# A spectral filter and a gated MLP on one core: loads on one queue, a gated spin, two-step roots, an inverse ordered by pairs

## The chip, the core and the metric

The kernel runs on one core of a Trainium2 chip. The metric is the device time of one execution in microseconds (us), as the median of several runs. TensorE (PE, with its weight loads PEld), VectorE (DVE), ScalarE (ACT), GpSimd (POOL) and SyncE (SP) each run their own instructions in a fixed order and wait for each other through semaphores. Loads and stores are DMAs; here SP, ACT and POOL issue them.

## The reference

```python
def reference(A_x, A_w_r, A_w_i, B_x, B_w_gate, B_w_up, B_w_down):
    x = A_x                                    # (1, 2048, 512), bf16
    xn = _layernorm(x, axis=-1)                # (x - mean) / sqrt(var + 1e-5)
    # A: irfft2(rfft2(xn) * (w_r + 1j * w_i)) over the two last axes
    # B: (gelu_tanh(xn @ w_gate) * (xn @ w_up)) @ w_down, inner width 1792
    return x + A + B
```

The comments stand for the bodies of two inner functions. All tensors are bf16.

## The kernel before, in words

The 2,048 tokens lie on 128 partitions with 16 tokens each; token `16 p + c` is partition p, column c. A "column" below is one c, that is 128 tokens of 512 values. Columns 0 to 3 form block 0, and so on to block 3.

**Layernorm.** Each column needs `bn_stats` and `bn_aggr` on DVE (L325, L328), a reciprocal root, and the normalised column `xn`. Columns 0 and 1 (`first_two`, L371) use ACT's square root and DVE's reciprocal, and are normalised in halves of 256 on DVE (L331). Columns 2 and 3 (`second_two`) run a root of Newton steps on DVE (`rsqrt_steps`, L342): two operations for a start value from the bits of the number, then three steps of three dependent operations. The later columns come four at a time (`later_four`): the same steps with four operations each on POOL, then ACT normalises (L449).

**Transposes.** Columns 0 to 3 are transposed on PE against the identity (L337) into PSUM and copied to `xnT` by DVE (L340). Columns 4 to 15 are transposed by DMAs on SP (L452).

**The MLP.** `unit` (L464) makes a gate product `g_ps` and an up product `u_ps` of four accumulating matmuls each (L483) for one 128-wide slice fc of the inner width and 1, 2 or 4 columns; ACT applies gelu (L488), DVE multiplies (L493, into `hT`). Columns 0 and 1 are done one at a time for fc 0 to 3, columns 0-1 and 2-3 in pairs after that, everything else in fours. `g_ps` and `u_ps` have two PSUM buffers each.

**The spectral part.** Four folds per block on DVE (L534, L540) feed 16 small matmuls against `RF_t` (`bp`, L552). Eight groups follow (`group`): matmuls `dp` and `ep`, a chain of DVE products with the filter (`TW`), an exchange of halves by four DMAs per group on SP (L702), and matmuls `gp` (L711). `inverse` (L736) takes pairs of columns: `yp` on PE (L742), a copy on ACT (L748), two sums `lv` and two `yt` on DVE (L754, L759).

**The end.** `down` (L776) accumulates 14 matmuls against `Wd_sb` (L787) and one of `yt` against `RI_t` (L791) into `y_ps` for each column; DVE adds x (L794), SP stores.

**What sets the order.** Loads are issued first, as written in L274 to L302: SP takes most of them, ACT takes the first three parts of the up weights and columns 2-3. Each load has one of eight semaphores in turn, so a load waits until the one eight places before it has landed. Then 37 spin matmuls on zeros are pinned at PE's head (L309). All later work goes through a planner (`Plan`, L124): each operation has an engine, an occupancy, a latency, dependencies, a key and buffers taken and given back; it is placed at the earliest modelled time. `LAND`, `W_LAND` and `RF_LAND` are the planner's assumed landing times. Only the order of each engine's instructions comes from it; the waits are those of the data and buffers.

Of the kernel before, what the change touches and what calls it, by code (L numbers as in the profile page):

```python
# [10 lines left out]
P = 128  # L11
# [10 lines left out]
NE = 4  # L22
# [3 lines left out]
EPS = 1e-5  # L26
N_SPIN = 37

# [93 lines left out]


class Op:  # L124
    __slots__ = ("eng", "occ", "lat", "fn", "deps", "key", "slack", "t_min", "acq", "rel", "start", "done", "n",
# [8 lines left out]
class Plan:  # L134
# [13 lines left out]
    def order(self):  # L148
        left = {}
        for op in self.ops:  # L150
            left.setdefault(op.eng, []).append(op)
        for ops in left.values():
            ops.sort(key=lambda o: (o.key, o.n))
        free = dict.fromkeys(left, 0.0)
        taken = dict.fromkeys(self.room, 0)
        back = {r: [] for r in self.room}
        out = []

        def start_of(op):
            if op.after is not None and op.after.start is None:  # L160
                return None
            t = max(free[op.eng], op.t_min)
            for d in op.deps:
                if d.done is None:
                    return None
                t = max(t, d.done + op.slack)
            for r in op.acq:
                over = taken[r] + 1 - self.room[r]
                if over > len(back[r]):
                    return None  # L170
                if over > 0:
                    t = max(t, sorted(back[r])[over - 1])
            return t

        while any(left.values()):
            best = None
            for eng, ops in left.items():
                pick = None
                for op in ops:
                    t = start_of(op)  # L180
                    if t is not None and (pick is None or t < pick[0] - 1e-6):
                        pick = (t, op)
                        if t <= free[eng] + 1e-6:
                            break
                if pick and (best is None or pick[0] < best[0]):
                    best = pick
            assert best, [(o.eng, o.key) for ops in left.values() for o in ops[:2]]
            t, op = best
            op.start, op.done = t, t + op.lat
            free[op.eng] = t + op.occ  # L190
            for r in op.acq:
                taken[r] += 1
            for r in op.rel:
                back[r].append(op.done)
            left[op.eng].remove(op)
            out.append(op)
        return out
# [3 lines left out]
def kernel(  # L201
# [74 lines left out]
    load_consts("ident", "ident")  # L276
    load_w(Wg_sb, 0, 256)
    load_w(Wg_sb, 256, 512)
    load_w(Wg_sb, 512, 1024)
    pin(load_w(Wu_sb, 0, 256, nc.scalar))  # L280
    pin(load_w(Wu_sb, 256, 512, nc.scalar))
    pin(load_x(2, 2, nc.scalar))
    pin(load_w(Wu_sb, 512, 1024, nc.scalar))
    load_x(4, 4)
    nc.sync.dma_start(out=RF_t[:], in_=rf_d.rearrange("p (c k) -> p c k", c=NC))
    load_w(Wg_sb, 1024, DF)
    load_w(Wu_sb, 1024, DF)
    load_x(8, 4)
    load_x(12, 4)
    load_consts("F0", "M0")  # L290
    LAND = {0: 3.0, 1: 3.4, 2: 7.4, 3: 7.4}
    LAND.update({c: 14.0 if c < 8 else 22.0 if c < 12 else 23.5 for c in range(4, NC)})
    W_LAND = [5.2] * 2 + [6.6] * 2 + [9.6] * 4 + [20.5] * 6
    RF_LAND, CT_LAND, TW_LAND = 15.5, 25.5, 29.0

# [11 lines left out]

    sp_ps = ps.tile([P, P], F32, name="sp_ps", tag="S", bufs=4)
    for _ in range(N_SPIN):  # L309
        pin(nc.tensor.matmul(sp_ps[:], lhsT=spin[:], rhs=spin[:], start=True, stop=True))  # L310

# [11 lines left out]
    def f_stats(c):  # L323
        tiles["st", c] = st = pw.tile([P, V.BN_STATS_DIM], F32, name="stats", bufs=3)
        V.bn_stats(out=st[:], in_=x_t[:, c, :])  # L325
# [12 lines left out]

    def f_Tc(c, e0, n):
        V.tensor_copy(out=xnT[0][:, e0:e0 + n, c, :], in_=tiles["T", c, e0][:])  # L340

    def rsqrt_steps(U, c0, n):  # L342
# [4 lines left out]
        def first():  # L347
            U.tensor_scalar(out=v[:], in0=mv[:, c0:c0 + n, 1], scalar1=EPS, scalar2=None, op0=ALU.add)
            U.tensor_scalar(out=y.bitcast(I32), in0=v[:].bitcast(I32), scalar1=-0.5, scalar2=float(0x5F3759DF),
                            op0=ALU.mult, op1=ALU.add)  # L350

        def newton():
            U.tensor_tensor(out=t[:], in0=y, in1=y, op=ALU.mult)
            if U is V:
                U.scalar_tensor_tensor(out=t[:], in0=v[:], scalar=-0.5, in1=t[:], op0=ALU.mult, op1=ALU.mult)
                U.scalar_tensor_tensor(out=y, in0=t[:], scalar=1.5, in1=y, op0=ALU.add, op1=ALU.mult)
                return
            U.tensor_tensor(out=t[:], in0=v[:], in1=t[:], op=ALU.mult)
            U.tensor_scalar(out=t[:], in0=t[:], scalar1=-0.5, scalar2=1.5, op0=ALU.mult, op1=ALU.add)
            U.tensor_tensor(out=y, in0=t[:], in1=y, op=ALU.mult)  # L360
# [5 lines left out]

        return [first, newton, newton, newton] + ([] if U is V else [bias])

    xn_op, xT_op = {}, {}

    def first_two():  # L371
        o = {}

        def v(k, fn, occ, deps=(), lat=None, t_min=0.0):
            o[k] = add("DVE", occ, fn, [o[d] for d in deps], key=-2000 + len(o), lat=lat, t_min=t_min)

# [5 lines left out]
        def T(c, h):  # L382
            o["T", c, h] = add("PE", 0.12, lambda: f_T(c, 2 * h, 2), [o["xn", c, h]], key=-2000 + 2 * c + h,
                               lat=0.4, acq=("S",))

# [18 lines left out]
        mean(0)  # L404
        stats(1)
        recip(0)
        xn_(0, 0)
        xn_(0, 1)
        mean(1)
        T(0, 0)  # L410
        T(0, 1)
        copy(0, 0)
        copy(0, 1)
        recip(1)
        xn_(1, 0)
# [12 lines left out]
    def moments(c, key):  # L428
        s = add("DVE", 0.7, lambda: f_stats(c), key=key, t_min=LAND[c], lat=0.7)
        return add("DVE", 0.1, lambda: f_mean(c), [s], key=key - 0.5)  # L430

    def second_two():
        m = [moments(c, -900 + c) for c in (2, 3)]
        for k, f in enumerate(rsqrt_steps(V, 2, 2)):
            m = [add("DVE", 0.4, f, m, key=-890 + k, lat=0.4)]
        for c in (2, 3):
            xn_op[c] = add("DVE", 0.33, lambda c=c: f_norm_v(c, 0, D), m, key=-880 + c)
            t = add("PE", 0.23, lambda c=c: f_T(c, 0, NE), [xn_op[c]], key=-880 + c, lat=0.5, acq=("S",))
            xT_op[c] = add("DVE", 0.34, lambda c=c: f_Tc(c, 0, NE), [t], key=-880 + c, rel=("S",))

    second_two()

    def later_four(c0, km, kx):
        m = [moments(c, km + 0.1 * c) for c in range(c0, c0 + 4)]
        for k, f in enumerate(rsqrt_steps(nc.gpsimd, c0, 4)):
            m = [add("POOL", (0.8, 1.15, 1.15, 1.15, 0.7)[k], f, m, key=c0 + k,
                     lat=(0.8, 1.15, 1.15, 1.15, 0.9)[k])]
        for c in range(c0, c0 + 4):
# [15 lines left out]
    def unit(k, c0, n, fc):  # L464
# [25 lines left out]
        def f_h():  # L490
            if alloc:
# [5 lines left out]
        g = add("PE", occ, lambda: mm("g_ps", "G", Wg_sb), src, key=1000 + k, lat=occ + 0.3, acq=("G",),  # L497
                t_min=W_LAND[fc])
        u = add("PE", occ, lambda: mm("u_ps", "U", Wu_sb), src, key=1000.5 + k, lat=occ + 0.3, acq=("U",),
                t_min=W_LAND[fc])  # L500
        ge = add("ACT", {1: 0.28, 2: 0.36, 4: 0.5}[n], f_ge, [g, table], key=-1000 + k,
# [98 lines left out]
    def group(i, g):  # L600
# [24 lines left out]
        for h in range(2):  # L625
            m = pe(0.224, lambda h=h: dp(h), bs_ops, kk + h, acq=("S",))
            m.t_min = 55.0 + 5.6 * i
            d = add("ACT", 0.5, lambda h=h: ds(h), [m], key=ka + 0.1 * h, acq=("ds",), rel=("S",))
# [98 lines left out]
    def load_ri():  # L727
        late["yt"] = pc.tile([P, NC, D], BF16, name="yt", tag="Bs")
        late["RI"] = pc.tile([P, NC, P], BF16, name="RI_t", tag="RF")
        nc.sync.dma_start(out=late["RI"][:], in_=ri_d.rearrange("p (c k) -> p c k", c=NC))  # L730

    ri = add("SP", 0.4, load_ri, gs_ops[-1:], key=300, lat=6.0)
    wd = add("SP", 0.4, lambda: nc.sync.dma_start(out=Wd_sb[:], in_=wd_v), key=50, lat=12.0, t_min=70.0)
    yt_op = {}

    def inverse(c0):  # L736
# [19 lines left out]

        def y(s):
            o = slice(511, 255, -1) if s else slice(0, 256)
            V.tensor_tensor(out=late["yt"][:, c0:c0 + 2, o], in0=b["lv"][:, :, 0], in1=b["lv"][:, :, 1],  # L759
                            op=ALU.subtract if s else ALU.add)  # L760

        d = []
        for j in range(2):
            m = pe(0.224, lambda j=j: yp(j), gs_ops, 1965 + 10 * (c0 + j), acq=("S",))
            d.append(add("ACT", 0.5, lambda j=j: yf(j), [m], key=60 + c0 + j, acq=() if j else ("E",), rel=("S",),
                         after=d[0] if d else None))
        d = [add("DVE", 0.35, lambda: lv(0), d + [ri], key=60 + c0, lat=0.35, acq=("X",))]
        d = [add("DVE", 0.42, lambda: lv(1), d, key=60 + c0 + 0.1, lat=0.42, rel=("E",))]
# [79 lines left out]
```

## Time and profile before

| what | us |
|---|---|
| median of three runs | 184.84 |
| lowest and highest of them | 184.56, 185.5 |
| the profiled execution's own time | 184.4 |
| its span, first to last instruction | 182.5 |
| PE busy | 174.2 (95%) |
| DVE busy | 119.0 (65%) |
| ACT busy | 96.5 (53%) |
| mean granted PE clock | 0.988 |

"Busy" is the union of an engine's instructions. Ends of matmuls are modelled and reach into the next ones, so a gap in PE's busy time is a little shorter than the time lost; starts of successive matmuls give the true rate. A wait is an idle stretch of an engine with what ended it. A line of a timeline gives start, length, engine, line of the kernel, operation, what it writes and reads, shapes, how many instructions are merged, and in brackets the idle time before it and who ended it. The granted clock is the share of PE's full clock. SPq and ACTq are the issuing of DMAs; their last number is the time from issue to landing. For this kernel the 40 slices of the page are 4.56 us each.

### The profile page before, as it was taken

How to read it: one execution, taken by the hardware profiler on the slowest of the kernel's cores; microseconds unless marked ns; L12 is line 12 of the kernel's file. 1: busy time of each engine (PE TensorE's matmuls, PEld its weight loads, DVE VectorE, ACT ScalarE, POOL GpSimd, SP SyncE). 2: the span in 40 equal slices, each digit the busy share in tenths (PEclk: the TensorE clock that was granted, in tenths of full speed). 3: DMA queues.
4: the chain of work that ended last, by engine and by line, in shares of the span. 5: the costliest groups of instructions: out<-in, count | busy, mean ns of one | idle time of the engine just before them, and what ended most of it. 6: DMA issues, size and time to landing. Idle time of an engine off the chain costs nothing.

```text
span 182.5 us, 3172 instructions
## 1 busy us (share of the span) xinstructions
PE 174.2 (95%) x1124; PEld 96.9 (53%) x1124; DVE 119.0 (65%) x279; ACT 96.5 (53%) x181; POOL 22.8 (12%) x68
## 2 busy tenths in 40 slices
PE   7497999999999999989999999999999999999993
PEld 7396774555455455545555545455544544544462
DVE  1687999895483499798999979637354254254221
ACT  3442437988947889988999965355211211121000
POOL 0000075588760000000000000000000000000000
PEclk9889999999999999999999999999999999999998
DMA  5999931442970002952211520230042222222221
GB/s 146 311 394 382 354 97 33 84 86 48 201 189 0 0 4 59 304 155 58 51 37 41 135 59 4 60 114 4 0 134 67 83 67 83 73 71 86 66 70 40
DMA packets 22208, 19.39 MB, mean 106 GB/s; under 512 B 8304, under 2 KB 20720, under 8 KB 22192
## 3 DMA queue, kind: packets, MB, share of 16 engines
q1 hardware_dynamic: 20048, 16.56, 30.3%
q0 software_dynamic: 416, 1.32, 3.1%
q10 hardware_dynamic: 1728, 1.31, 2.3%
q8 instruction: 9, 0.15, 0.3%
q14 instruction: 7, 0.06, 0.1%
HBM read 13.41 MB, written 2.10 MB: 85 GB/s over the span
## 4 chain that ended last, share of the span: by engine, by line
PE 82%; DMA 11%; DVE 4%; issue 1%; SPq 0%; DVEq 0%
PE y_ps L787 27%; PE u_ps L483 23%; PE g_ps L483 22%; DMA Wu_sb<-in_B_w_up_dram 6%; DMA F<-F 3%; DMA x_t<-in_A_x_dram 2%; PE yp L742 2%; PE bp L552 2%; PE gp L711 2%; PE y_ps L791 2%; DVE hT L493 2%; PE dp L608 1%; PE ep L617 1%; DVE xnT L340 0%; DVE m L658 0%
## 5 line engine op out<-in xcount | busy, mean ns | idle before, releaser
L483 PE MATMUL u_ps<-xnT,Wu_sb 128*128 128x512 bf16 (+2 forms) x272 | 59.2, 345 | 1.0 <-DMA Wu_sb<-in_B_w_up_dram 1.0
L483 PE MATMUL g_ps<-xnT,Wg_sb 128*128 128x512 bf16 (+2 forms) x272 | 59.5, 347 | 0.3 <-DVE xnT L340 0.3
L493 DVE TENSOR_TENSOR hT<-u_ps,ge 128x512 bf16<-128x512 f32 (+2 forms) x68 | 39.9, 592 | 20.1 <-PE u_ps L483 12.4
L787 PE MATMUL y_ps<-Wd_sb,hT 128*128 128x512 bf16 (+1 forms) x238 | 51.1, 366 | 0.0
L488 ACT ACTIVATE ge<-g_ps 128x512 bf16<-128x512 f32 (+2 forms) x68 | 35.6, 525 | 26.9 <-PE g_ps L483 22.8
L483 PEld LDWEIGHTS <-Wg_sb 128*128 128x128 bf16 x272 | 25.8, 101 | 21.2 <-DVE xnT L340 0.6
L483 PEld LDWEIGHTS <-Wu_sb 128*128 128x128 bf16 x272 | 25.5, 100 | 21.6 <-DMA Wu_sb<-in_B_w_up_dram 1.3
L787 PEld LDWEIGHTS <-hT 128*128 128x128 bf16 x238 | 22.8, 98 | 22.4
L794 DVE TENSOR_TENSOR y_sb<-y_ps,y_sb 128x512 bf16<-128x512 f32 (+1 forms) x17 | 11.1, 660 | 30.5 <-PE y_ps L791 30.5
L748 ACT CAST yf<-yp 128x512 bf16<-128x512 f32 x16 | 9.1, 589 | 34.4 <-PE yp L742 32.3
L622 ACT CAST E<-ep 64x512 bf16<-64x512 f32 x32 | 18.5, 579 | 1.5 <-PE ep L617 1.1
L325 DVE BATCH_NORM_STATS2 stats<-x_t 128x6 f32<-128x512 bf16 x16 | 10.7, 672 | 4.7 <-DMA x_t<-in_A_x_dram 4.7
L449 ACT ACTIVATE xn<-x_t,nb,rstd 128x512 bf16<-128x512 bf16 x12 | 9.4, 819 | 2.2 <-POOL nb L365 2.2
L522 ACT CAST Gs<-gp 128x512 bf16<-128x512 f32 x16 | 9.0, 594 | 1.0 <-PE gp L711 0.9
L522 ACT CAST ds<-dp 128x512 bf16<-128x512 f32 x16 | 9.0, 597 | 0.0
L522 ACT CAST Bs<-bp 128x512 bf16<-128x512 f32 x16 | 8.2, 604 | 0.0
L754 DVE TENSOR_TENSOR lv<-yf 128x512 bf16<-128x512 bf16 x16 | 6.1, 421 | 1.3 <-ACT yf L748 0.6
L742 PEld LDWEIGHTS <-Gs 128*128 128x128 bf16 x64 | 4.7, 98 | 3.1
L711 PEld LDWEIGHTS <-F 128*128 128x128 bf16 x64 | 4.4, 98 | 3.5 <-DMA F<-F 1.0
L759 DVE TENSOR_TENSOR yt<-lv 128x512 bf16<-128x512 bf16 x16 | 6.1, 421 | 0.3
L791 PE MATMUL y_ps<-yt,RI_t 128*128 128x512 bf16 (+1 forms) x17 | 6.1, 366 | 0.0
L711 PE MATMUL gp<-CT,F 128*128 128x128 bf16 x64 | 5.5, 219 | 0.5 <-DMA F<-F 0.5
(64 smaller groups left out, 124.9 us busy)
## 6 DMA issues: line engine op xcount, KB each, us to landing
F<-F SPq DMA_DIRECT2D x32, 64.0 KB, 2.0
y_sb<-in_A_x_dram SPq DMA_DIRECT2D x16, 128.0 KB, 2.1
out_dram<-y_sb SPq DMA_DIRECT2D x15, 128.0 KB, 1.7
Wd_sb<-in_B_w_down_dram SPq DMA_DIRECT2D x1, 1792.0 KB, 8.4
x_t<-in_A_x_dram SPq DMA_DIRECT2D x3, 512.0 KB, 11.0
Wg_sb<-in_B_w_gate_dram SPq DMA_DIRECT2D x1, 768.0 KB, 10.3
Wu_sb<-in_B_w_up_dram SPq DMA_DIRECT2D x1, 768.0 KB, 10.1
Wu_sb<-in_B_w_up_dram ACTq DMA_DIRECT2D x2, 256.0 KB, 4.7
```

The source lines that it names most:

```text
L325: V.bn_stats(out=st[:], in_=x_t[:, c, :])
L449: xn_op[c] = add("ACT", 0.72, lambda c=c: A.activation(out=xn[:, c, :], in_=x_t[:, c, :], func=AF.Identity, bias=nb[:, c:c + 1], scale=rst ...
L483: T_.matmul(b[name][:], lhsT=W_[:, e, fc * P:(fc + 1) * P], rhs=rhs[:, e, :], start=(e == 0), stop=(e == NE - 1))
L488: A.activation(out=b["ge"][:], in_=b["g_ps"][:], func=AF.Gelu_apprx_tanh)
L493: V.tensor_tensor(out=hT[sb, fc][:, o:o + w], in0=b["u_ps"][:], in1=b["ge"][:], op=ALU.mult)
L522: A.copy(out=o, in_=i)
L622: A.copy(out=b["E"][64 * h:64 * h + 64, r], in_=b["ep", h][64 * r:64 * r + 64])
L711: T_.matmul(t[:, q], lhsT=b["F2"][:, h, q % 2, q // 2::2], rhs=cc("M" if 2 * g + h else "M0"), start=(q == 0), stop=(q == 3), skip_group_c ...
L748: A.copy(out=b["yf"][:, j], in_=b[j][:])
L787: T_.matmul(b[o][:], lhsT=hT[sb, f][:, cl * P:(cl + 1) * P], rhs=Wd_sb[:, f, o:o + w], start=(f == 0), stop=False)
L791: T_.matmul(b[o][:], lhsT=late["RI"][:, c, :], rhs=late["yt"][:, c, o:o + w], start=False, stop=True)
L794: V.tensor_tensor(out=b["y"][:, o:o + w], in0=b[o][:], in1=b["y"][:, o:o + w], op=ALU.add)
```

## The change

1. All opening loads are issued by SP: columns 0, 1, the identity, columns 2-3, then gate and up weights in alternating parts, then columns 4-7, the rest of the weights, columns 8-11, `RF_t`, columns 12-15 and the constants. ACT issues none. `RF_t` moves behind columns 8-11. The planner's assumed landing times change with it.
2. The 37 spin matmuls of 128 columns become 20 of them and 5 of 512 columns that read column 0 of x.
3. The reciprocal root has two steps (other constants) in place of three, on DVE and on POOL.
4. In `first_two`, DVE's order is fixed: statistics and mean of column 0, the same of column 1, then the reciprocals and normalisations. Copies of transposed columns 2 and 3 go to ACT. `bn_stats` results have four buffers, not three.
5. The planner counts a dependency on the same engine by the engine's occupancy (PE, DVE) and not by latency.
6. `RI_t` is loaded after the last `bp` has been copied, not after the last `gp`; the buffer of `yt` is taken when `yt` is first written.
7. `yp` of both columns of the first pair have one key; those of later pairs have keys 20 higher, so each later `yp` stands two columns later on PE than before. In the resulting order the second `yp` of a pair stands just ahead of the 14 matmuls of the pair's first column.

Without the spin both programs have the same 1,087 matmuls.

```diff
-N_SPIN = 37
+SAME = {"PE": 0.0, "DVE": 0.09}
...
-                t = max(t, d.done + op.slack)
+                t = max(t, d.start + d.occ + SAME[op.eng] if d.eng == op.eng and d.eng in SAME else d.done + op.slack)
...
     load_consts("ident", "ident")
-    load_w(Wg_sb, 0, 256)
-    load_w(Wg_sb, 256, 512)
-    load_w(Wg_sb, 512, 1024)
-    pin(load_w(Wu_sb, 0, 256, nc.scalar))
-    pin(load_w(Wu_sb, 256, 512, nc.scalar))
-    pin(load_x(2, 2, nc.scalar))
-    pin(load_w(Wu_sb, 512, 1024, nc.scalar))
+    load_x(2, 2)
+    for f0, f1 in ((0, 256), (256, 512), (512, 1024)):
+        load_w(Wg_sb, f0, f1)
+        load_w(Wu_sb, f0, f1)
     load_x(4, 4)
-    nc.sync.dma_start(out=RF_t[:], in_=rf_d.rearrange("p (c k) -> p c k", c=NC))
     load_w(Wg_sb, 1024, DF)
     load_w(Wu_sb, 1024, DF)
     load_x(8, 4)
+    nc.sync.dma_start(out=RF_t[:], in_=rf_d.rearrange("p (c k) -> p c k", c=NC))
     load_x(12, 4)
...
-    sp_ps = ps.tile([P, P], F32, name="sp_ps", tag="S", bufs=4)
-    for _ in range(N_SPIN):
-        pin(nc.tensor.matmul(sp_ps[:], lhsT=spin[:], rhs=spin[:], start=True, stop=True))
+    sp_ps = ps.tile([P, D], F32, name="sp_ps", tag="S", bufs=4)
+    for k in range(25):
+        pin(nc.tensor.matmul(sp_ps[:, :P if k < 20 else D], lhsT=spin[:], rhs=spin[:] if k < 20 else x_t[:, 0, :],
+                             start=True, stop=True))
...
-        return [first, newton, newton, newton] + ([] if U is V else [bias])
+        steps = [first, lambda: newton(0.703952253, 0.703952253 * 2.38924456), lambda: newton(0.5, 1.5)]
+        return steps + ([] if U is V else [bias])
...
         stats(0)
         mean(0)
         stats(1)
+        mean(1)
         recip(0)
         xn_(0, 0)
         xn_(0, 1)
-        mean(1)
+        recip(1)
         T(0, 0)
         T(0, 1)
         copy(0, 0)
         copy(0, 1)
-        recip(1)
...
-            xT_op[c] = add("DVE", 0.34, lambda c=c: f_Tc(c, 0, NE), [t], key=-880 + c, rel=("S",))
+            xT_op[c] = add("ACT", 0.5, lambda c=c: f_Tc(c, 0, NE, A.copy), [t], key=-1100 + c, rel=("S",))
...
-    ri = add("SP", 0.4, load_ri, gs_ops[-1:], key=300, lat=6.0)
+    ri = add("SP", 0.4, load_ri, bs_ops[-1:], key=300, lat=6.0, t_min=60.0)
...
-            m = pe(0.224, lambda j=j: yp(j), gs_ops, 1965 + 10 * (c0 + j), acq=("S",))
+            m = pe(0.224, lambda j=j: yp(j), gs_ops, 1985 + 10 * (c0 + j) if c0 else 1990, acq=("S",))
...
-        d = [add("DVE", 0.35, lambda: lv(0), d + [ri], key=60 + c0, lat=0.35, acq=("X",))]
+        d = [add("DVE", 0.35, lambda: lv(0), d, key=60 + c0, lat=0.35, acq=("X",))]
```

More of the change, by code (lines that the diff above doesn't have):

```diff
@@ L288 @@
     load_x(8, 4)
+    nc.sync.dma_start(out=RF_t[:], in_=rf_d.rearrange("p (c k) -> p c k", c=NC))
     load_x(12, 4)
     load_consts("F0", "M0")
[L291 to L294, printed above, removed]
+    LAND = {0: 3.0, 1: 3.4, 2: 4.3, 3: 4.3}
+    LAND.update({c: 12.6 if c < 8 else 18.5 if c < 12 else 21.5 for c in range(4, NC)})
+    WG_LAND = [5.2] * 2 + [7.0] * 2 + [9.5] * 4 + [15.0] * 6
+    WU_LAND = [6.1] * 2 + [7.9] * 2 + [11.0] * 4 + [17.0] * 6
+    RF_LAND = 20.0
     idx_t = pc.tile([P, 3], I32, name="idx_t")
@@ L323, in f_stats @@
     def f_stats(c):
-        tiles["st", c] = st = pw.tile([P, V.BN_STATS_DIM], F32, name="stats", bufs=3)
+        tiles["st", c] = st = pw.tile([P, V.BN_STATS_DIM], F32, name="stats", bufs=4)
         V.bn_stats(out=st[:], in_=x_t[:, c, :])
@@ L337, in f_T, with f_Tc @@
             T_.transpose(tp[:, e], xn[:, c, (e0 + e) * P:(e0 + e + 1) * P], ident)
-    def f_Tc(c, e0, n):
-        V.tensor_copy(out=xnT[0][:, e0:e0 + n, c, :], in_=tiles["T", c, e0][:])
+    def f_Tc(c, e0, n, copy=V.tensor_copy):
+        copy(out=xnT[0][:, e0:e0 + n, c, :], in_=tiles["T", c, e0][:])
     def rsqrt_steps(U, c0, n):
@@ L348, in first, with newton @@
             U.tensor_scalar(out=v[:], in0=mv[:, c0:c0 + n, 1], scalar1=EPS, scalar2=None, op0=ALU.add)
-            U.tensor_scalar(out=y.bitcast(I32), in0=v[:].bitcast(I32), scalar1=-0.5, scalar2=float(0x5F3759DF),
+            U.tensor_scalar(out=y.bitcast(I32), in0=v[:].bitcast(I32), scalar1=-0.5, scalar2=float(0x5F1FFFF9),
                             op0=ALU.mult, op1=ALU.add)
-        def newton():
+        def newton(a, k):
             U.tensor_tensor(out=t[:], in0=y, in1=y, op=ALU.mult)
             if U is V:
-                U.scalar_tensor_tensor(out=t[:], in0=v[:], scalar=-0.5, in1=t[:], op0=ALU.mult, op1=ALU.mult)
-                U.scalar_tensor_tensor(out=y, in0=t[:], scalar=1.5, in1=y, op0=ALU.add, op1=ALU.mult)
+                U.scalar_tensor_tensor(out=t[:], in0=v[:], scalar=-a, in1=t[:], op0=ALU.mult, op1=ALU.mult)
+                U.scalar_tensor_tensor(out=y, in0=t[:], scalar=k, in1=y, op0=ALU.add, op1=ALU.mult)
                 return
             U.tensor_tensor(out=t[:], in0=v[:], in1=t[:], op=ALU.mult)
-            U.tensor_scalar(out=t[:], in0=t[:], scalar1=-0.5, scalar2=1.5, op0=ALU.mult, op1=ALU.add)
+            U.tensor_scalar(out=t[:], in0=t[:], scalar1=-a, scalar2=k, op0=ALU.mult, op1=ALU.add)
             U.tensor_tensor(out=y, in0=t[:], in1=y, op=ALU.mult)
@@ L374, in v @@
         def v(k, fn, occ, deps=(), lat=None, t_min=0.0):
-            o[k] = add("DVE", occ, fn, [o[d] for d in deps], key=-2000 + len(o), lat=lat, t_min=t_min)
+            o[k] = add("DVE", occ, fn, [o[d] for d in deps], key=-2000 + len(o), lat=lat, t_min=t_min,
+                       after=o.get("last"))
+            o["last"] = o[k]
         def root_of(c):
@@ L383, in T @@
             o["T", c, h] = add("PE", 0.12, lambda: f_T(c, 2 * h, 2), [o["xn", c, h]], key=-2000 + 2 * c + h,
-                               lat=0.4, acq=("S",))
+                               lat=0.36, acq=("S",))
         def recip(c):
@@ L428, in moments @@
     def moments(c, key):
-        s = add("DVE", 0.7, lambda: f_stats(c), key=key, t_min=LAND[c], lat=0.7)
+        s = add("DVE", 0.6, lambda: f_stats(c), key=key, t_min=max(LAND[c], 6.4))
         return add("DVE", 0.1, lambda: f_mean(c), [s], key=key - 0.5)
@@ L434, in second_two @@
         for k, f in enumerate(rsqrt_steps(V, 2, 2)):
-            m = [add("DVE", 0.4, f, m, key=-890 + k, lat=0.4)]
+            m = [add("DVE", 0.4, f, m, key=-890 + k, lat=0.42)]
         for c in (2, 3):
@@ L445, in later_four @@
         for k, f in enumerate(rsqrt_steps(nc.gpsimd, c0, 4)):
-            m = [add("POOL", (0.8, 1.15, 1.15, 1.15, 0.7)[k], f, m, key=c0 + k,
-                     lat=(0.8, 1.15, 1.15, 1.15, 0.9)[k])]
+            m = [add("POOL", (0.8, 1.15, 1.15, 0.7)[k], f, m, key=c0 + k,
+                     lat=(0.8, 1.15, 1.15, 0.9)[k])]
         for c in range(c0, c0 + 4):
@@ L497, in unit @@
         g = add("PE", occ, lambda: mm("g_ps", "G", Wg_sb), src, key=1000 + k, lat=occ + 0.3, acq=("G",),
-                t_min=W_LAND[fc])
+                t_min=WG_LAND[fc])
         u = add("PE", occ, lambda: mm("u_ps", "U", Wu_sb), src, key=1000.5 + k, lat=occ + 0.3, acq=("U",),
-                t_min=W_LAND[fc])
+                t_min=WU_LAND[fc])
         ge = add("ACT", {1: 0.28, 2: 0.36, 4: 0.5}[n], f_ge, [g, table], key=-1000 + k,
@@ L626, in group @@
             m = pe(0.224, lambda h=h: dp(h), bs_ops, kk + h, acq=("S",))
-            m.t_min = 55.0 + 5.6 * i
+            m.t_min = 54.0 + 5.5 * i
             d = add("ACT", 0.5, lambda h=h: ds(h), [m], key=ka + 0.1 * h, acq=("ds",), rel=("S",))
@@ L727, in load_ri @@
     def load_ri():
-        late["yt"] = pc.tile([P, NC, D], BF16, name="yt", tag="Bs")
         late["RI"] = pc.tile([P, NC, P], BF16, name="RI_t", tag="RF")
         nc.sync.dma_start(out=late["RI"][:], in_=ri_d.rearrange("p (c k) -> p c k", c=NC))
-    ri = add("SP", 0.4, load_ri, gs_ops[-1:], key=300, lat=6.0)
+    ri = add("SP", 0.4, load_ri, bs_ops[-1:], key=300, lat=6.0, t_min=60.0)
     wd = add("SP", 0.4, lambda: nc.sync.dma_start(out=Wd_sb[:], in_=wd_v), key=50, lat=12.0, t_min=70.0)
@@ L757, in y @@
         def y(s):
+            if s + c0 == 0:
+                late["yt"] = pc.tile([P, NC, D], BF16, name="yt", tag="Bs")
             o = slice(511, 255, -1) if s else slice(0, 256)
```

## The prediction

> **What bounds the kernel now.** I read the page's engine rows first, then who waited for whom, then TensorE's and VectorE's timelines of the first 19 us, the stretches, and the DMA issues.
>
> ```profile
> PE 174.2 (95%) x1124; PEld 96.9 (53%) x1124; DVE 119.0 (65%) x279; ACT 96.5 (53%) x181; POOL 22.8 (12%) x68
> PE   7497999999999999989999999999999999999993
> DVE  1687999895483499798999979637354254254221
> ```
>
> TensorE (PE) is the bound, with holes only in the first four slices, one in slice 18 and the store at the end.
>
> ```profile
> PE tp L337 <- DVE xn L331: 2.4, 1, 2.4
> PE u_ps L483 <- DMA Wu_sb<-in_B_w_up_dram: 1.0, 1, 1.0
> PE gp L711 <- DMA F<-F: 0.5, 1, 0.5
> PE g_ps L483 <- DVE xnT L340: 0.3, 1, 0.3
> ```
>
> These are all of PE's waits after the spin; the stretches show where the clock is lost as well (columns: length, PE busy, granted clock, DMA):
>
> ```profile
> 7.03:10.86 3.83, 3.77 (x34) 0.56 1.04 359
> 10.86:18.77 7.91, 6.59 (x82) 1.00 1.05 389
> 18.77:80.00 61.23, 61.23 (x392) 1.00 0.45 117
> 80.00:81.50 1.50, 1.00 (x14) 1.00 0.01 3
> 81.50:179.30 97.80, 97.80 (x573) 1.00 0.22 65
> ```
>
> So outside the opening only 80 to 81.5 us has room. The opening in order:
>
> ```profile
> 0.98 3.68 PE L310 MATMUL sp_ps<-spin 128*128 128x128 bf16 x37 [0.98 <-DVE eps_t L263]
> 3.10 0.69 DVE L325 BATCH_NORM_STATS2 stats<-x_t 128x6 f32<-128x512 bf16 x1 [2.17 <-DMA x_t<-in_A_x_dram]
> 5.24 0.69 DVE L325 BATCH_NORM_STATS2 stats<-x_t 128x6 f32<-128x512 bf16 x1 [1.45 <-DMA x_t<-in_A_x_dram]
> 5.85 0.30 DVE L328 BATCH_NORM_AGGREGATE mv<-stats 128x2 f32<-128x6 f32 x2
> 6.64 0.84 DVE L331 TENSOR_SCALAR xn<-x_t,mv,rstd 128x256 bf16<-128x256 bf16 x3
> 7.03 1.36 PE L337 MATMUL tp<-CT,xn 128*128 128x128 bf16 x8 [2.37 <-DVE xn L331]
> 8.18 0.63 PE L483 MATMUL g_ps<-xnT,Wg_sb 128*128 128x128 bf16 x4
> 15.64 1.05 PE L483 MATMUL u_ps<-xnT,Wu_sb 128*128 128x256 bf16 x8 [1.00 <-DMA Wu_sb<-in_B_w_up_dram]
> ```
>
> Column 0's mean is queued behind column 1's statistics, and these wait for a load that lands at 5.24; so PE has nothing from 4.66 to 7.03. The clock then drops and the first matmuls take 107 ns per 128 columns.
>
> **PE's account.** The order of instructions of both kernels holds the same 1,087 matmuls besides the spin: 336 of 128 columns, 126 of 256, 625 of 512. At full clock, start to start, they take 55.5 ns (16 in 0.89), 109 ns and 215.8 ns (14 in 3.02): 18.6 + 13.7 + 134.9 = 167.3 us. From 7.03 that would end at 174.3; the last one ends its issue at 179.2. Lost after the first transpose: 4.9 us. It splits so: first transpose to first g, 1.15 less 0.44 of work = 0.7; half clock from 8.18 to 10.86, 25 matmuls too long by 51 ns = 1.3; the wait for the up weights 1.2 (the view's 1.0 counts from a modelled end); the wait for xnT 0.5 and small ones 0.1; the exchange at 80.6 in two steps 0.9; evacuation before y_ps at 124.7, 0.2.
>
> **First columns.** x0, x1, ident, x2-3 and the weights now go out in this order on SP alone. With SP's issue spacing of 0.43 us, x1 should land half a microsecond after x0, not 2.1. Bounds for x0: no later than 3.08 as now; no earlier than about 2.5, by when 128 KB would have moved at the present total rate (26 KB to 2.0, then 193 KB in one us). Statistics, mean, root now run per column: statistics of column 1 from about 3.5 to 3.9, +0.6 statistics, +0.15 mean, +0.25 reciprocal to xn, +0.39 to the first transpose (6.64 to 7.03): 4.9 to 5.35, I take 5.1. The gated spin costs nothing before that: 20 cold matmuls fill 0.98 to 3.1, five of 512 columns at 0.43 end at 5.25 if all are cold and near 4.7 if the clock rises at 4.0. Bounds 0 to 0.2. Gain 7.03 - 5.1 = 1.9.
>
> **Clock.** The row first: PE stood idle 2.37 us and the clock was 0.50 from about 7.45 to 10.86. The Trainium skill, "TensorE: Matmul & The Clock Gate", Part 1, says throttling takes an idle window of about 3.4 us. By that rule the present gap shouldn't have cooled the array, the longer spin would be worth nothing, and my sum would lose 1.2 us. The trace shows cooling after a window that was about 30% busy (0.6 of spin, 0.4 of transposes), while the one holding the stall at 14.7 to 15.6, about 70% busy, kept the clock. In the changed kernel the gap shrinks to under 1.5 us with transposes inside, so any 3.4 us is some 60 to 70% busy: I side with the row and take 0.1 of cold loss (bounds 0 and 1.3). Gain 1.2.
>
> **Weights.**
>
> ```profile
> Wg_sb<-in_B_w_gate_dram SPq DMA_DIRECT2D x1, 512.0 KB, 8.0
> Wu_sb<-in_B_w_up_dram ACTq DMA_DIRECT2D x1, 512.0 KB, 10.4
> ```
>
> Issued at 5.24, the up half landed at 15.6. The skill's "DMA: Bandwidth & Descriptors", Queues, rings and completion order, says each DMA engine takes turns between queues by packet; that fits an ACT queue of 1 KB rows trickling beside SP's 4 KB rows[...]. By the rates of each us in the trace (cumulative 0.48 MB at 4, 1.07 at 6, 1.67 at 8, 2.39 at 10, 2.80 at 11, 3.98 at 14, 4.73 at 16) the new order lands x2-3 near 4.3, up columns 0-255 at 6.0, to 511 at 7.7, to 1023 at 10.6, the rest at 16. PE asks for them at about 6.2, 7.7, 11.4 and 22. If 512-byte rows alone in one queue run at 250 GB/s instead of 300, the first two slip by up to 1 us. I take 0.15 of the 1.2 as left: gain 1.05.
>
> **VectorE (DVE) in the opening.** This is what is late next. From the first g at 5.8 until columns 2-3 are normalised it must do, start to start: 2 statistics 1.2, 4 copies 0.8, 2 xn halves 0.4, 8 hT of 128 columns 1.7, 2 means 0.2, 8 dependent root steps 1.6 (0.2 each as at 12.15 to 14.19; the third Newton step's 0.6 is gone), 2 xn 0.6: 6.5, to 12.2. PE's own work up to the transposes of 2-3 (16 + 4 groups, 8 transposes) is 5.7, to 11.5. In the order, statistics stand ahead of two hT products three times, and u matmuls wait for a PSUM buffer behind them: walking both queues I get waits of 0.1 to 0.3, in all 0.9, and PE's first 512-column group at 21.6 with 14.9 of work behind it. Bounds: 0.5 (the present 0.5 + 0.1, DVE being equally loaded then) to 2.0. Against the present 0.6 this is 0.3 worse. The two copies moved to ACT (0.41 each there on DVE) and the lost Newton step are in this sum. After that DVE, 97 to 99% busy from 18.8 to 32 us now, gets earlier by its idle pieces now filled (1.45, 1.09, 0.96) and 1.3 of work taken off: 4.8, enough for PE's lead of about 4.1, with margins of 0.5 to 1 us. I add 0.1.
>
> **Things at no cost.** POOL's shorter roots (1.1 us less per group of four) bring ACT's xn and the DMA transposes forward; PE reaches xnT1 at about 33.8, transposes issued from about 23, 6.4 us in all, are done before; without that cover they'd cost their lag. ACT gets two 0.5 us copies and loses four issues; it has 3 us idle there. RF and constants land by 19 and 21, used at 25. RI now waits on SP for the last bp matmul (near 48), ahead of the first exchange (near 65): 3.7 us of loading, hidden. The fourth stats buffer removes waits only.
>
> **Exchange at 80.6.**
>
> ```profile
> 69.28 2.44 SPq L702 DMA_DIRECT2D F<-F  x4
> 71.77 0.59 SPq L733 DMA_DIRECT2D Wd_sb<-in_B_w_down_dram  x1
> 75.15 2.40 SPq L702 DMA_DIRECT2D F<-F  x4
> ```
>
> The second exchange waits behind Wd (8.4 us). SP's order is unchanged there, so all of it comes 4 us earlier, but its gp now stands at 70.3 us of PE work instead of 69.0: 1.3 us of cover for a loss of 0.9. Left 0.2 (bounds 0 and 0.9): gain 0.7.
>
> **Inverse by pairs.** Each second yp comes just before a block of 14 y_ps. From yp's end (131.7) to the pair's last yt (134.14) it now takes 2.5 us; the matmul that needs it comes after 3.02 + 0.22 = 3.24. Taken as nothing; below nothing is excluded but for the 0.2 at 124.7, since PE is dense there. The tail is the same.
>
> **Sum.** 5.1 + 167.3 + (0.65 + 0.1 + 0.15 + 0.9 + 0.1 + 0.2 + 0.15) = 174.6 against 179.2: 4.6 less. Span 182.5 becomes 177.9; with the 1.9 around it the profiled run's 184.4 becomes 179.8. The median of the three runs is 184.84, 0.4 above the profiled one, part of it likely the clock's phase; I say 180.0.
>
> **Rivals.**
> - *The opening stays starved* (15%): DVE's order or 512-byte loads make PE wait 2 us rather than 0.9 + 0.15. For it: DVE 11.5 of 15.7 us busy there and every u behind it. Against: the present opening has the same load with waits of 0.5. Time 181.2.
> - *The clock still drops* (8%): only transposes and early g fill the window after the spin. Its 1.2 comes back: 181.2.
> - *The lead isn't kept* (5%): DVE is the bound to 32 us, and only the load waits are gained: PE falls back by 2.5: 182.5.
> - *Slower than before* (2%): the pairs. If copy, lv and yt take over 3.24 us, each of seven pairs stalls PE by the excess; beyond 3.24 + 4.6/7 = 3.9 us per pair the gain is gone; at 4.1 the time is about 186. Against: 2.5 measured, with DVE's total (0.69) already ahead of it.
> - *As worked out* (70%): 180.0, own range 179.1 to 181.0.
>
> About 0.5% (0.9 us) is what a measurement tells from no change. Below 183.9 lie the sum and three rivals: faster 0.95; within, 0.03 (the lead lost and the exchange worse); slower 0.02. Range 178.9 to 181.8, of which the upper end takes in starved loads or a cold clock.
>
> **What would show it.** Right: first transpose at 5.1 +- 0.3, clock 1.00 from 5 us on, no PE wait on Wu_sb over 0.3, first 512-column group near 21.6, gp's second group without a wait, ri matmuls without waits. Wrong: a stretch at 0.5 after 6 us, PE waits on hT or u of over 1.5 us before 22, an xnT wait at 33, or waits of y_ps L796 on yt.

## The result and the profile after

The changed kernel takes 183.06 us (median of 4, 182.57 to 183.82), the kernel before 185.09 beside it (184.56 to 185.5): ratio 0.9895, 95% interval 0.9851 to 0.994. The profiled execution took 183.08 with a span of 181.2. So it is faster, by 2.0 us where 4.8 were forecast, and the time lies above the range. Times of one kernel differ by up to 1.8 us between chips, so times are compared on one chip only.

The engine rows and TensorE's waits of the changed kernel:

```profile
PE 173.6 (96%) x1112; PEld 96.2 (53%) x1112; DVE 117.5 (65%) x274; ACT 98.5 (54%) x183; POOL 18.7 (10%) x56
PE   7599999998899999999999999999999999999992
...
PEclk9789999999999999999999999999999999999999
```

```profile
PE g_ps L487 <- DMA Wg_sb<-in_B_w_gate_dram: 1.0, 1, 1.0
...
PE g_ps L487 <- issue: 0.6, 1, 0.6
PE u_ps L487 <- DVE hT L497: 0.6, 1, 0.6
PE u_ps L487 <- DMA Wu_sb<-in_B_w_up_dram: 0.5, 1, 0.5
PE tp L338 <- DVE xn L332: 0.5, 1, 0.5
```

The wait for xn is 0.5 instead of 2.4, the exchange (gp) waits no more, and the up weights' wait of 1.0 near 15 us is gone. New are 1.5 us for the first weights, and a hole near slice 10; the dip of the clock is still there. The opening in order of time:

```profile
2.87 0.69 DVE L326 BATCH_NORM_STATS2 stats<-x_t 128x6 f32<-128x512 bf16 x1 [1.94 <-DMA x_t<-in_A_x_dram]
3.70 0.66 DVE L326 BATCH_NORM_STATS2 stats<-x_t 128x6 f32<-128x512 bf16 x1
5.06 0.54 PE L338 MATMUL tp<-CT,xn 128*128 128x128 bf16 x4 [0.45 <-DVE xn L332]
6.64 0.40 PE L487 MATMUL g_ps<-xnT,Wg_sb 128*128 128x128 bf16 x4 [1.04 <-DMA Wg_sb<-in_B_w_gate_dram]
7.51 0.61 PE L487 MATMUL u_ps<-xnT,Wu_sb 128*128 128x128 bf16 x4 [0.47 <-DMA Wu_sb<-in_B_w_up_dram]
```

Column 1's statistics no longer wait for their load, and the first transpose stands at 5.06. Then both first products wait for weights. The stretches (length, PE busy, clock, DMA share, GB/s) of the changed kernel, and below them of the kernel before:

```profile
2.00:3.00 1.00, 1.00 (x13) 1.00 0.84 247
3.00:4.00 1.00, 1.00 (x6) 1.00 0.73 192
4.00:5.00 1.00, 0.61 (x3) 1.00 0.66 159
5.00:6.00 1.00, 0.54 (x4) 1.00 0.92 259
3.65:7.06 3.41, 1.90 (x13) 1.00 0.91 255
7.06:10.48 3.42, 2.97 (x29) 0.50 1.13 333
```

```profile
2.00:3.00 1.00, 1.00 (x13) 1.00 0.70 193
3.00:4.00 1.00, 1.00 (x12) 1.00 0.89 257
4.00:5.00 1.00, 0.66 (x11) 1.00 1.10 322
5.00:6.00 1.00, 0.00 (x0) 1.00 1.14 304
4.04:7.45 3.41, 1.04 (x14) 1.00 1.06 302
```

From 3 to 6 us one queue moved 192, 159 and 259 GB/s where two had moved 257, 322 and 304. After a stretch of 3.41 us of which 1.90 were busy, the clock was halved for the next 3.42. (Before the clock's first record, here at 3.65, this view prints 1.00, though the spin's 20 matmuls of 128 columns took 105 ns each, as at half clock.)

By the prediction's own account (starts of all matmuls less 167.3 us of work), the lead-in and losses before the last matmul come to 10.25 us instead of 7.35:

| term | forecast | measured |
|---|---|---|
| first transpose | 5.1 | 5.06 |
| to the first u, with the waits for weights | 0.8 | 2.0 |
| half clock | 0.1 | 1.4 |
| VectorE to 32 us | 1.0 | 0.2 |
| near 44 us | 0 | 1.5 |
| exchange and rest | 0.35 | 0.1 |

With 0.4 more behind the last matmul (3.7 instead of 3.3, see the third step below) these differences make up the 3.3 us between the profiled 183.08 and the forecast's 179.8.

### The profile page after: what moved, and what is told of

Its sections match the earlier page's. It is cut to its first block, busy times and chain, and to the rows that moved or that the text cites. A ratio compares the mean times of both kernels' runs of the same rounds, so it can differ in the third digit from the quotient of the medians.

```text
span 181.2 us, 3134 instructions
## 1 busy us (share of the span) xinstructions
PE 173.6 (96%) x1112; PEld 96.2 (53%) x1112; DVE 117.5 (65%) x274; ACT 98.5 (54%) x183; POOL 18.7 (10%) x56
## 4 chain that ended last, share of the span: by engine, by line
PE 93%; DMA 2%; SPq 1%; DVE 1%; issue 0%
PE u_ps L487 28%; PE y_ps L792 27%; PE g_ps L487 26%; DMA Wu_sb<-in_B_w_up_dram 2%; PE dp L612 2%; PE gp L715 2%; PE yp L745 2%; PE bp L556 2%; PE y_ps L796 2%; PE ep L621 2%; SPq L268 1%; PE tp L338 0%; DVE hT L497 0%; SPq L272 0%; DVE y_sb L799 0%
## 5 line engine op out<-in xcount | busy, mean ns | idle before, releaser
L487 PE MATMUL g_ps<-xnT,Wg_sb 128*128 128x512 bf16 (+2 forms) x272 | 58.8, 346 | 1.6 <-DMA Wg_sb<-in_B_w_gate_dram 1.0
L487 PEld LDWEIGHTS <-Wg_sb 128*128 128x128 bf16 x272 | 25.4, 100 | 21.6 <-DMA Wg_sb<-in_B_w_gate_dram 1.2
L745 PE MATMUL yp<-CT,Gs 128*128 128x128 bf16 x64 | 6.0, 219 | 0.0
```

Source lines behind the costliest of these rows:

```text
L487: T_.matmul(b[name][:], lhsT=W_[:, e, fc * P:(fc + 1) * P], rhs=rhs[:, e, :], start=(e == 0), stop=(e == NE - 1))
L745: T_.matmul(t[:, q], lhsT=late["G"][:, q, c0 + j], rhs=IQ[q], start=(q == 0), stop=(q == 3), skip_group_check=True)
```

## Experiments

Seventeen runs on five chips (A to E). The kernel before took 185.59, 184.04, 184.09, 183.76 and 185.29 us on them.

**Chip A: does it repeat, and what makes the opening wait?** The changed kernel unaltered:

> The changed kernel again, unaltered: it tells what repeats. Theory A (loads and clock in the opening are the kernel's own, the loss at 44 us is an event of one run): first transpose near 5.1, g waits for the gate weights about 1.0 and u about 0.5, clock 0.50 from 7 to 10.5, no wait over 0.3 near 44 us; time 181.5. Theory B (the loss at 44 us comes of the gathers, which now start at 36 instead of 43): the 1.6 us are back between 40 and 46 us; time 183.0.

183.46 us (ratio to before 0.9858, 0.9807 to 0.9908). All came back: first transpose 5.25, waits of 1.4 and 0.3 for weights, clock 0.50 from 7.25 to 10.67, and the waits of 0.56 and 0.57 at 44.61 and 46.20. So the loss near 44 us is no single event, which theory A had said.

Columns 2 and 3 behind the first weights:

```diff
-    load_x(2, 2)
     for f0, f1 in ((0, 256), (256, 512), (512, 1024)):
         load_w(Wg_sb, f0, f1)
         load_w(Wu_sb, f0, f1)
+        if f0 == 0:
+            load_x(2, 2)
```

> Only the load of columns 2 and 3 is moved behind the first pair of weights on the same queue. Theory A (256 KB of tokens stand ahead of the weights in one queue): the first gate weights land near 5.7 instead of 6.6 and the up weights near 6.5, the first g follows the transposes within 0.2 us, and the opening is 1.0 to 1.4 us shorter up to the second u; if the window from 3.6 to 7 us is then busy enough the clock stays at 1.00 and another 1.2 us go. Time 1.0 to 2.4 us below the changed kernel. Rival (the queue is slow in the first 6 us, whatever stands in it): weights land after 6.3, time within 0.4 us of the changed kernel.

182.81 us (0.9846, 0.9793 to 0.9899), 0.65 below the changed kernel, between what the two theories had said. The first weights landed at 5.65 and 6.38, the first g came at 6.07 without a wait, and the clock stayed at 1.00. But the second pair was now what came late:

```profile
8.61 0.62 PE L488 MATMUL g_ps<-xnT,Wg_sb 128*128 128x128 bf16 x8 [1.03 <-DMA Wg_sb<-in_B_w_gate_dram]
9.88 0.62 PE L488 MATMUL u_ps<-xnT,Wu_sb 128*128 128x128 bf16 x8 [0.66 <-DMA Wu_sb<-in_B_w_up_dram]
```

The wait of 1.5 moved and became 1.7. Both theories are half right: the order decides which matmul waits. That the bytes of one queue in the first 8 us decide how long is my reading of this one run.

Filler matmuls in front of the two waits; `filler(n)` issues n matmuls of 512 columns whose results are unused:

```diff
             T_.transpose(tp[:, e], xn[:, c, (e0 + e) * P:(e0 + e + 1) * P], ident)
+        if c == 0 and e0 == 2:
+            filler(4)
...
+            if k == 0 and name == "g_ps":
+                filler(2)
```

> Six matmuls of 512 columns on the spin tile are put in front of the two waits for weights (four behind the second transposes of column 0, two behind the first g); no other edit, results unused. Theory A (the clock fell because the window before 7 us was half empty): clock 1.00 from about 4 us on, weights land as before, time 1.0 to 1.3 us below the changed kernel. Rival (the window counts transposes or a few idle stretches otherwise, or the clock falls by its own schedule): clock 0.50 from 7 to 10.5 as before, and the time is the same or up to 0.8 us above, since cold filler matmuls take 0.43 us each.

182.22 us (0.9817, 0.9771 to 0.9862), 1.2 below the changed kernel: theory A. The stretch behind the first rise of the clock, with fillers and with the columns late:

```profile
4.55:7.96 3.41, 3.18 (x29) 1.00 1.02 302
```

```profile
3.76:7.17 3.41, 2.60 (x25) 1.00 0.95 268
```

In both the clock stayed at 1.00 to the end of the matmuls.

The loads on two queues as before, all else changed:

> The load issues of the kernel before (gate weights on SP, up weights and columns 2 and 3 on ACT) with all else as changed. Theory A (one queue brought the early first transpose and took away the late up weights, and cost the first gate weights 1.0): first transpose near 6.8, PE waits 1.0 to 1.5 for up weights near 15, first g without a wait for weights; time 1.0 to 2.0 us above the changed kernel. Rival (the split of the queues hardly matters, most of the gain comes from the rest of the change): within 0.5 us of the changed kernel.

184.79 us (0.9969, 0.9947 to 0.9991), 1.3 above the changed kernel: theory A in size. From 3 to 6 us its two queues (first view; the last number is GB/s) moved more than the one queue of the unaltered kernel on this chip (run again, second view):

```profile
3.00:4.00 1.00, 0.50 (x4) 1.00 0.69 215
4.00:5.00 1.00, 1.00 (x3) 1.00 1.15 342
5.00:6.00 1.00, 1.00 (x3) 1.00 1.18 299
```

```profile
3.00:4.00 1.00, 1.00 (x6) 1.00 0.97 193
4.00:5.00 1.00, 0.70 (x4) 1.00 0.60 156
5.00:6.00 1.00, 0.54 (x4) 1.00 0.93 275
```

With the columns late, one queue moved 117, 307 and 277, so what stands in it counts too. The first transpose stood at 6.47, and the clock first rose at 9.75. What theory A had wrong: the up weights near 15 us cost 0.2, not 1.0 to 1.5. Instead VectorE stood 1.81 us at column 2's statistics, whose load came at 9.74 on the second queue, and hT and a u matmul (0.92) waited behind them.

**Chip B: the loss near 44 us, the roots, the pairs.** The changed kernel itself was not run on this chip. The row list of GpSimd's gathers is loaded behind the last transpose:

```diff
-    nc.sync.dma_start(out=idx_t[:], in_=nc.inline_tensor(idx_np, name="spec_rows").ap())
+    idx_d = nc.inline_tensor(idx_np, name="spec_rows").ap()
...
-    tw = add("POOL", 7.5, tables_gather, key=40, lat=12.0, t_min=42.0)
+    ix = add("SP", 0.4, lambda: nc.sync.dma_start(out=idx_t[:], in_=idx_d), [xT_op[15]], key=16, lat=2.0)
+    tw = add("POOL", 5.0, tables_gather, [ix], key=40, lat=5.0, t_min=42.0)
```

> The load of the gathers' row list stands behind the last transpose on SP, so that GpSimd's six gathers start near 49 us instead of 36; all other queues keep their order. Theory A (the loss of 1.6 us near 44 us comes from the gathers while TensorE's groups wait for ScalarE and VectorE): ge and hT get TensorE's results on time between 41 and 45 us, no wait of g or u there, and the profiled execution is 1.4 to 1.6 us shorter than the changed kernel's with its clock (span 179.6 to 180.1); the gathers end near 57, used at 64. If they cost the same wherever they stand, the loss turns up 8.2 us behind their start, near 57. Rival (the loss is made by something else near 42 us): the waits of 0.56 and 0.6 stay near 44 us.

181.81 us (0.9866, 0.9807 to 0.9924), span 179.3, no wait near 44 or 57, gathers from 48.87 to 56.3. It looked like theory A, but without the changed kernel beside it that isn't shown; see the pairs below.

With the fillers as well:

> The six filler matmuls of the earlier run and the late gathers together. If both causes are independent, their gains add: clock 1.00 from 4 us on and no wait near 43 us, span about 1.5 us under the 180.4 of the fillers alone, 178.8 to 179.3, time 180.4 to 181.0. Rival (the loss moves with the gathers or the lead is used up later): span 180.0 to 180.5.

180.93 us (0.9821, 0.9775 to 0.9866), span 179.1, clock 1.00: the lowest median of all, though on C the late gathers added nothing to the fillers.

A third step in GpSimd's roots:

```diff
+        if U is not V:
+            last = steps[2]
+            steps[2] = lambda: (last(), last())
         return steps + ([] if U is V else [bias])
```

> GpSimd does a third Newton step again in each of its three roots (the last step twice), all queues otherwise in the changed kernel's order. The gathers then start about 1.8 us later, near 37.9. Theory A (loss bound to the gathers): the waits of TensorE stay, 8.2 us behind the gathers' start, near 46, total the same; time within 0.5 us of the changed kernel, plus what later transposes cost. Rival (bound to the place in the schedule): the waits stay at the same groups near 44 us.

183.47 us (0.9958, 0.9935 to 0.9982). Neither theory: the gathers started at 39.28, g and u wait nowhere near 44 us, and there are 1.2 us of other waits (2.1 by the starts of the matmuls). ScalarE's queue of this kernel, then TensorE's:

```profile
39.15 0.81 ACT L456 ACTIVATE xn<-x_t,nb,rstd 128x512 bf16<-128x512 bf16 x1 [3.52 <-POOL nb L366]
39.87 1.54 ACT L529 CAST Bs<-bp 128x512 bf16<-128x512 f32 x3
```

```profile
40.48 1.36 PE L559 MATMUL bp<-RF_t,xf 128*128 128x128 bf16 x12 [0.66 <-ACT Bs L529]
42.43 0.38 PE L559 MATMUL bp<-RF_t,xf 128*128 128x128 bf16 x4 [0.59 <-ACT Bs L529]
```

ScalarE stands 3.52 us at the normalisation that waits for the root, the casts that empty TensorE's PSUM buffers stand behind it, and TensorE waits for those. With two steps the same wait is 1.14 (in the run with the pairs undone) and nothing comes late. The third step also takes back the 0.4 us behind the last matmul: 3.3 here and in both profiles of the kernel before, 3.7 in all sixteen with two steps. It lies in the closing exchange of semaphores, where GpSimd's second event follows its first by 0.09 us with three steps and by 0.45 with two; why is open.

The inverse in its old order (first argument of the pairs' key back to `1965 + 10 * (c0 + j)`):

> Only the order of the inverse is put back to that of the kernel before: the first yp matmuls of each pair are no longer held back. Theory (the pairs are worth the 0.2 us of the wait at the start of the inverse, and cost nothing): a wait of 0.1 to 0.3 before a y_ps group near 124 us comes back, nothing else moves. Rival (yp in pairs costs waits of y_ps later on): the time falls by up to 0.5 us.

182.39 us (0.9882, 0.982 to 0.9944). By the starts of the matmuls, 0.2 us are lost before y_ps at 122.3, as before the change: the theory. The run gave more: its gathers ran from 36.46 as in the changed kernel, and TensorE lost nothing near 44. So what chip A lost there isn't owed to the early gathers alone.

**Chips C to E: two by two, and the loss again.**

> The changed kernel once more, beside the late gathers on one chip: the run with the pairs undone had its gathers at 36.5 us and lost nothing near 44, on another chip than the runs that lost 1.6 there. Theory A (the early gathers cost 1.6 us wherever the kernel runs): waits of g and u near 44 us. Rival (the loss belongs to that chip or to chance): none here, or not in every run.

> Late gathers beside the changed kernel on one chip. Theory A: 1.3 to 1.7 us shorter than the changed kernel of this call at the same clock. Rival (chip or chance): within 0.4 us of it.

> The fillers alone on the same chip. Theory: clock near 1.00 in every run, where the changed kernel shows 0.99 in two runs of three; median 1.0 to 1.4 us below the changed kernel of this call. Rival: clock 0.99 in some runs, median within 0.5.

> Both on the same chip. Theory A: the two gains add, 2.4 to 3.0 us below the changed kernel of this call. Rival (the gathers cost nothing on this chip): as the fillers alone within 0.4.

On C: 181.73 (0.9856, 0.9817 to 0.9896), 182.43 (0.9896, 0.9854 to 0.9937), 181.18 (0.9834, 0.9799 to 0.9869), 181.25 us (0.9836, 0.9798 to 0.9873). No kernel lost anything near 44 us; theory A fell for this chip, and late gathers bring nothing. The fillers brought 0.5 in the median, less than the 1.0 to 1.4 expected; the four runs of the changed kernel with a mean clock of 0.99 took 181.72 to 182.54, the two at 1.00 took 180.96 and 181.01.

> The changed kernel, to see whether this chip shows the loss near 44 us at all: then TensorE's g and u wait 0.5 to 1.3 us there; if not, nothing is told apart.

> If the chip shows the loss: theory A (early gathers): no wait near 44 us and none elsewhere up to 64; theory B (the loss follows the gathers): waits 7 to 9 us behind their start, near 57; rival (the place in the schedule or the chip alone): the waits stay near 44 us.

> The kernel before on this chip. Theory A and B (gathers at 43 us, between 43 and 52): B expects waits of TensorE near 51, A none; the rival expects that a loss of 1 to 2 us shows somewhere between 40 and 55 us also here.

On D: 182.14, 181.87 and 184.07 us, no loss in any of the three: nothing told apart.

> As before: shows whether this chip has the loss near 44 us (waits of g and u of 0.5 to 1.3) or not; so far one chip of four had it.

> If the chip has the loss: none near 44 under the theory that the early gathers make it, waits near 57 if it follows them, the same waits near 44 if it is the place or the chip. If the chip does not have it: the same as the changed kernel.

On E: 182.29 (0.9834, 0.9806 to 0.9863) and 182.0 us (0.9819, 0.979 to 0.9847), and here the changed kernel shows the loss, at a full clock:

```profile
40.98 1.03 PE L487 MATMUL g_ps<-xnT,Wg_sb 128*128 128x512 bf16 x4
42.76 0.60 ACT L492 ACTIVATE ge<-g_ps 128x512 bf16<-128x512 f32 x1 [1.09 <-PE g_ps L487]
43.40 1.02 PE L487 MATMUL g_ps<-xnT,Wg_sb 128*128 128x512 bf16 x4 [0.54 <-issue]
44.28 0.69 DVE L497 TENSOR_TENSOR hT<-u_ps,ge 128x512 bf16<-128x512 f32 x1 [4.04 <-PE u_ps L487]
45.02 1.02 PE L487 MATMUL u_ps<-xnT,Wu_sb 128*128 128x512 bf16 x4 [0.59 <-DVE hT L497]
```

The same stretch with the late gathers on this chip:

```profile
42.25 0.67 ACT L492 ACTIVATE ge<-g_ps 128x512 bf16<-128x512 f32 x1
42.95 0.69 DVE L497 TENSOR_TENSOR hT<-u_ps,ge 128x512 bf16<-128x512 f32 x1 [1.96 <-ACT ge L492]
43.46 1.03 PE L487 MATMUL g_ps<-xnT,Wg_sb 128*128 128x512 bf16 x4
```

TensorE's rows run on evenly, but ScalarE and VectorE hear of its groups 1.4 to 3.0 us late: a group's semaphore event comes 0.39 us after the start of its last matmul elsewhere in this trace, but those of the four groups whose last matmuls start at 39.90, 40.76, 41.62 and 42.48 come at 42.73, 44.19, 44.24 and 44.30. Once the two PSUM buffers of g and of u are full, TensorE waits for ge and hT. The first gather was issued at 35.22, the last from 41.91 to 42.85. With the gathers from 49.34 these groups were heard of on time, but the lag had moved with the gathers:

```profile
56.44 0.61 PE L613 MATMUL dp<-CT,Bs 128*128 128x128 bf16 x8
57.87 1.07 ACT L526 CAST ds<-dp 128x512 bf16<-128x512 f32 x2 [1.50 <-PE dp L613]
```

Here ds follows dp by 1.43 us, on B with the same late gathers by 0.42. So two groups are heard of 1.0 us late, 8.5 us after the first gather (in the changed kernel the late events came 7.5 to 9.1 after it). This cost TensorE only 0.17 us. The two medians still differ by only 0.3 us: in this one profile the opening with the late gathers came 0.5 later, and from 22 to 80 us it lost 0.7 in small waits, the 0.17 among them, against 0.1 beside the loss of 1.5 in the other. In the profiles with the lag, events of ScalarE and VectorE are missing from the record while the gathers run (up to seven and three), on B, C and D none. So whether their signals were late too isn't known, and a part of the recording itself in the lag isn't excluded.

## Why the prediction was wrong, by its steps

- **First columns: right.** 5.1 forecast, 5.06 measured. Undoing the queue alone puts the transpose at 6.47 and costs 1.3 us.
- **Weights: the step that failed.** The landing times were read off the bytes that two queues had moved together in the kernel before, as if one queue moved as much and each transfer had all of it to itself. Columns 2-3 and the three parts of the up weights landed at 5.57, 7.46, 9.25 and 12.23 (by the events of their semaphores) where 4.3, 6.0, 7.7 and 10.6 stood. Two errors in it. From 2 to 5 us the single queue moved 0.60 MB where the two had moved 0.77, and on chip A the same shows with only the issue of the loads changed. And summed bytes aren't the bytes of the transfer that is waited for. The first gate weights and what stood ahead of them are 0.82 MB (128, 128, 32, 256 and 256 KB); when they had landed, at 6.60, about 1.09 MB had moved since the start (0.03 to 2 us and the rows above, with 335 GB/s from 6 us): transfers behind them were already under way. The working gives these weights no time of their own; by its bytes I estimate 5.2. They came 0.5 us earlier than in the kernel before (7.12), but the first g now wanted them near 5.9 and not at 8.2. So there were waits of 1.5 us instead of 0.15; the "slip by up to 1 us" was seen as a risk, but 0.15 went into the sum. The Trainium skill, "DMA: Bandwidth & Descriptors", Queues, rings and completion order, speaks of how an engine takes turns between queues, and no rate of a lone queue follows from that. (The cumulative bytes from 6 us on are also 0.03 MB too low, worth 0.1 us.)
- **Clock: failed, as a consequence.** "Any 3.4 us is some 60 to 70% busy": with the weights' wait it was 56% (1.90 of 3.41), and the rival "the clock still drops", given 8%, is what happened. Of the 20 runs of the changed kernel, the result's four included, 12 show a mean of about 0.99 and eight don't; with the fillers none of 24 does. So the cooling comes of the empty opening; in the profiled run it cost 1.4 us by the starts of the matmuls from 7.51 to 10.48.
- **Near 44 us: not foreseen.** "Things at no cost" let GpSimd's shorter roots be free. With the earlier opening they moved the gathers from 43 to 36 us. In every profile with early gathers on chips A and E, and in the result's, TensorE lost 1.5 us there; on B, C and D in none of five. Late gathers moved the lag with them on E, in one profile, to where it cost 0.2. That the gathers take part is thus supported, on such chips; why those chips, and why the signals come late, stays open. On A the late gathers weren't run.
- **Roots: the hidden cost was the wrong way round.** They aren't free of effect: without them, in this order of the queues, TensorE loses 1.2 us (2.1 by starts) behind ScalarE's wait. The cover that I named (the transposes' lead) wasn't what mattered; the casts behind the waiting normalisation were. In the kernel before, whose order was planned for three steps, TensorE had no such wait, though ScalarE waited 2.2 us for these roots. And the two steps go with 0.4 us more behind the last matmul, where the prediction said "the tail is the same".
- **VectorE in the opening: over-sized.** 0.9 and 0.1 forecast, 0.2 measured; probably because TensorE came to it later, its first 512-column group at 23.6 instead of 21.6. With a full clock two profiles show a wait at 22 us, of 0.4 (gather_late on B) and 0.3 (on E), the others none.
- **Exchange and pairs: right.** No wait of gp in the profiled run, 0 to 0.45 in others, against 0.2; the pairs bring 0.2 and cost nothing.

So the mechanisms of gain held. Three costs, of together 4.0 us more than forecast, and the 0.4 behind the last matmul weren't in the sum or were sized too small; that 1.1 were sized too large hid a part of this by luck.

## What to carry to other kernels

Time a transfer by what stands ahead of it in its own queue and by the rate of such a queue at that moment, not by the bytes that all queues moved together. A stage that wakes TensorE early must also feed it: an opening that starts 2 us sooner and then waits for weights gives the time back twice, once as the wait and once as a cold clock, and here six filler matmuls bought the second part back, 1.2 us on chip A and 0.5 on C. Where a step off the path gets shorter, follow what it releases (here the gathers) and what waits in order behind it (here the casts).

## What the runs showed of the hardware

- **The clock moves in stretches of 3.41 us.** In all profiled runs but three it first rises somewhere from 3.65 to 6.3 us, and it either falls 3.41 us later or stays. The eight stretches after which it fell were busy for 1.04 to 1.90 us (transposes counted), the eleven after which it stayed for 1.73 to 3.41: from 1.97 on none fell, but 1.73 stayed once, so the share alone doesn't decide. No gap within them was longer than 2.4 us. The Trainium skill, "TensorE: Matmul & The Clock Gate", Part 1, gives an idle window of about 3.4 us as the condition; here half-empty ones were enough. A mean clock of 1.00, which counts the time before the first record as full clock, can also hide a clock that rises only at 10.23 us, as in the kernel before and the changed one on chip D: look at the stretch, not at the mean.
- **Signals can lag.** On chip E four of TensorE's groups, 0.86 us apart, were signalled 1.4 to 3.0 us late, three of them within 0.11 us, while its own rows ran on evenly; with the gathers 14 us later, two groups near 57 us were late by 1.0.
- **Chips differ.** The same kernel before took 183.8 to 185.6 us, and the two slowest chips are the ones with the loss near 44 us.
